# One burst of small-tile products per batch, at the boundary of its output tiles

## The chip, the cores and the metric

The kernel runs on one NeuronCore of a Trainium2 chip. The metric is the device time in microseconds. A NeuronCore has a matrix engine (TensorE, PE in the profile, with its weight loads listed as PEld), a vector engine (VectorE, DVE), a scalar engine (ScalarE, ACT), a general engine (GpSimd, POOL) and a queue engine for transfers (SyncE, SP). Products of TensorE land in PSUM, which has eight banks of 128 x 512 fp32 here; DVE and ACT copy them out.

## The reference

Two parts follow each other. A two-way cross attention between 512 tokens and 32 state rows, for 8 batches and 8 heads of width 64:

```python
scores  = x @ state.T / sqrt(D);  a  = softmax(scores);   xread = a  @ state   # 512 rows a batch
scores2 = state @ x.T / sqrt(D);  a2 = softmax(scores2);  sread = a2 @ x       # 32 rows a batch
attn = concat([xread, sread], axis=2)          # (B, H, 544, 64)
```

Then a feed-forward layer on all 8 x 544 rows of width 512 (the heads side by side): `gelu(rows @ w_in) @ w_out`, with an inner width of 2048.

## The kernel before

The kernel never forms `xread`. It multiplies the state with `w_in` first, `P = state @ w_in` for each head, and then takes `a @ P` for the hidden values. So a batch consists of:

- P: per batch four chunks of 512 hidden columns. The state of one head is 64 x 32, so a product uses a 64 x 32 part of the array (a "small tile"), and eight of them, four heads on each of two row halves, run side by side. A chunk fills two PSUM banks (t = 0, 1).
- `mm1`: the hidden tiles `hp`, full-array products, followed by a Gelu on ACT (16 per batch).
- `mm2`: the output tiles `op`, full-array products. A batch has four output tiles (j) of four quarters each (q), 16 steps; after q = 3, DVE copies the tile out (`evac`).
- `sread`: the read-out for the state rows, also on small tiles (128 x 32), and `srt`, its transpose.

PSUM is two pools of four banks:

```python
ps_f = ctx.enter_context(tc.tile_pool(name="ps_f", bufs=4, space=PSUM))
ps_o = ctx.enter_context(tc.tile_pool(name="ps_o", bufs=4, space=PSUM))
ctx.enter_context(tc.manual_schedule())
```

Each pool gives its banks out in turn, and each engine executes its instructions in the order of the program text. Here are the helpers that the change and the prediction touch:

```python
    def sread(b):
        A = atts[b]
        pool, tag = (ps_f, "f") if b < 2 else (ps_o, "op")
        A.sr = pool.tile([128, 2, 65], FP32, name="sr", tag=tag)
        for t in range(2):
            for j in range(SJ):
                for c in range(HC):
                    nc.tensor.matmul(
                        A.sr[32 * c:32 * c + 32, t, :],
                        lhsT=A.e[:, 2 * j + t, 32 * c:32 * c + 32],
                        rhs=A.xo[:, j, c, 1 + 65 * t:66 + 65 * t],
                        start=(j == 0),
                        stop=(j == SJ - 1),
                    )

    def sread_out(b):
        A = atts[b]
        A.srm = att.tile([128, 2, D], BF16, name="srm", tag="srm")
        flat = A.sr.rearrange("q t d -> q (t d)")
        inv = att.tile([128, 2], FP32, name="inv", tag="inv")
        nc.vector.reciprocal(out=inv, in_=flat[:, 0:130:129])
        nc.vector.tensor_tensor(
            out=A.srm,
            in0=flat[:, 1:129].rearrange("q (t d) -> q t d", t=2),
            in1=inv[:, :].to_broadcast((128, 2, D)),
            op=ALU.mult,
        )

    def pmat(b, fs, act=()):
        if b not in Ps:
            Ps[b] = att.tile([128, 2, d_ff], BF16, name="P", tag="P")
        pss = []
        for f in fs:
            pool, tag = (ps_o, "op") if b == 0 and f == 0 else (ps_f, "f")
            ps = [pool.tile([128, 512], FP32, name="p_ps", tag=tag) for t in range(2)]
            for c in range(HC):
                for t in range(2):
                    nc.tensor.matmul(
                        ps[t][32 * c:32 * c + 32, :],
                        lhsT=sbd[64 * t:64 * t + 64, b, c, 32 * t:32 * t + 32],
                        rhs=w_in_bf[64 * t:64 * t + 64, c, f * 512:(f + 1) * 512],
                        start=True,
                        stop=True,
                    )
            pss.append(ps)
        for f, ps in zip(fs, pss):
            for t in range(2):
                dst = Ps[b][:, t, f * 512:(f + 1) * 512]
                if t in act:
                    nc.scalar.copy(out=dst, in_=ps[t])
                else:
                    nc.vector.tensor_copy(out=dst, in_=ps[t])

    def mm1(b, m):
        if m == 0:
            gs[b] = gpool.tile([128, MC, S], BF16, name="g", tag="g")
        hp = ps_f.tile([128, S], FP32, name="hp", tag="f")
        for t in range(2):
            nc.tensor.matmul(
                hp,
                lhsT=Ps[b][:, t, m * 128:(m + 1) * 128],
                rhs=atts[b].AT[:, :, t, :],
                start=(t == 0),
                stop=(t == 1),
            )
        nc.scalar.activation(out=gs[b][:, m, :], in_=hp, func=AF.Gelu)

    ops = {}

    def evac(ps, rows):
        osb = opool.tile([128, d_model], FP32, name="osb", tag="osb")
        nc.vector.tensor_copy(out=osb, in_=ps)
        for r, src in rows:
            nc.sync.dma_start(out=r, in_=osb[src, :])

    # mm2(b, q, j), without its first lines
        if q == 0:
            ops[b, j] = ps_o.tile([128, d_model], FP32, name="op", tag="op")
        ps = ops[b, j]
        for m in range(4 * q, 4 * q + 4):
            nc.tensor.matmul(
                ps,
                lhsT=gs[b][:, m, j * 128:(j + 1) * 128],
                rhs=w_out_bf[:, m, :],
                start=(m == 0),
                stop=(m == MC - 1),
            )
        if q == 3:
            evac(ps, [(out_rows(b, j), slice(0, 128))])

    def M(*ms):
        for m in ms:
            mm1(m // MC, m % MC)

    def U(*us):
        for u in us:
            mm2(u // 16, u % 16 // 4, u % 4)
```

`scores(nb, half)` makes the scores of the next batch in `ps_f` and takes their exponential on ACT; `norm(nb, half)` is a sum, a reciprocal and a multiplication on DVE. The end of the prologue and the main loop:

```python
    # ... prologue cut
    M(16)
    pmat(1, (1,), act=(1,))
    U(13)
    M(17)
    U(14)
    pmat(1, (2,), act=(1,))
    M(18)
    U(15)
    M(19)


    u = 16
    for b in range(1, B):
        nb = b + 1
        for p in range(2 if b == 1 else 0, 8):
            k = 16 * b + 2 * p
            if p == (4 if b == 1 else 1) and nb < B:
                scores(nb, 0)
                scores(nb, 1)
                if b == 1:
                    norm(nb, 0)
                    norm(nb, 1)
            if b > 1 and p in (2, 3) and nb < B:
                norm(nb, p - 2)
            if p == (7 if b == 1 else 4) and nb < B:
                atr_dma(nb)
            if p == 5 and nb + 1 < B:
                begin(nb + 1)
                rearr(nb + 1)
                xtr_dma(nb + 1)
                rearr_ones(nb + 1)
            M(k, k + 1)
            if nb == B and p >= 4:
                for m in range(4 * p - 16, 4 * p - 12):
                    mm1_sr(m)
            while u < k - 4 - (b == 1 and p == 3):
                U(u)
                u += 1
            if b == 1 and p == 3:
                pmat(b, (3,), act=(1,))
                U(u)
                u += 1
            if b > 1 and p == 2:

                sread(b)
                pmat(b, (2, 3), act=(1,))
                sread_out(b)
            if p == 6 and nb < B:
                pmat(nb, (0, 1), act=(1,))
                if b + 3 < B:


                    nc.gpsimd.tensor_copy(out=hold, in_=Ps[nb][:, 0, 0:1])
                    load_x(b + 3)
            if p == 2 and b > 1 or p == 6 and nb < B:
                U(u, u + 1)
                u += 2
            if p == 3 and b > 1:
                srt(b)
```

The step U(u) runs four hidden tiles behind M, so the last output tile of batch b - 1 (u = 16 b - 1) ends in step p = 2 of batch b.

Of the kernel before, what the change touches and what calls it, by code (L numbers as in the profile page):

```python
# [9 lines left out]
FP32 = mybir.dt.float32  # L10
# [7 lines left out]
def kernel(  # L18
# [8 lines left out]
    nc = tc.nc  # L27

    B, H, S, D = x.shape
# [4 lines left out]
    HC = H // 2  # L34
# [10 lines left out]
    ps_f = ctx.enter_context(tc.tile_pool(name="ps_f", bufs=4, space=PSUM))  # L45
    ps_o = ctx.enter_context(tc.tile_pool(name="ps_o", bufs=4, space=PSUM))
# [5 lines left out]
    w_in_bf = persist.tile([128, HC, d_ff], BF16, name="w_in_bf")  # L52
    w_out_bf = persist.tile([128, MC, d_model], BF16, name="w_out_bf")
    ident = persist.tile([128, 128], BF16, name="ident")
    sbd = persist.tile([128, B, HC, 2 * NS], BF16, name="sbd")
# [6 lines left out]
    hold = persist.tile([128, 1], BF16, name="hold")  # L62
# [9 lines left out]
    for c in range(3):  # L72
# [5 lines left out]
        out=xbs[0].rearrange("p (t c) f -> p t c f", t=2)[:, :, 3, :], in_=x0_rows[:, :, 3, :]  # L78
# [22 lines left out]
    def load_x(b):  # L101
        xb = xin.tile([128, H, SJ * D], BF16, name="xb", tag="xb")
        nc.gpsimd.dma_start(out=xb, in_=xr[b])
        xbs[b] = xb
# [55 lines left out]
    def begin(b):  # L160
        A = Att()
        atts[b] = A
        A.x4 = x4s[b % 2]
        A.xo = xos[b % 2]
        A.xT = att.tile([128, SJ, HC, 128], BF16, name="xT", tag="xT")
        A.e = att.tile([128, SJ * 2, HC * NS], BF16, name="e", tag="e")
        A.a = att.tile([128, SJ * 2, HC * NS], BF16, name="a", tag="a")
# [117 lines left out]
    def norm(b, half):  # L285
        A = atts[b]
        G = SJ * 2
        hs = slice(64 * half, 64 * half + 64)
        e4 = A.e[:, :, hs].rearrange("p g (c n) -> p g c n", n=NS)
        cs = att.tile([128, G, 2], FP32, name="cs", tag="cs")  # L290
        nc.vector.reduce_sum(out=cs, in_=e4, axis=AX.X)  # L291
        ics = att.tile([128, G, 2], FP32, name="ics", tag="ics")
        nc.vector.reciprocal(out=ics, in_=cs)
        nc.vector.tensor_tensor(  # L294
            out=A.a[:, :, hs].rearrange("p g (c n) -> p g c n", n=NS),
            in0=e4,
            in1=ics[:, :, :].to_broadcast((128, G, 2, NS)),
            op=ALU.mult,
        )
# [20 lines left out]

    def sread(b):
        A = atts[b]
        pool, tag = (ps_f, "f") if b < 2 else (ps_o, "op")
        A.sr = pool.tile([128, 2, 65], FP32, name="sr", tag=tag)
        for t in range(2):
            for j in range(SJ):
                for c in range(HC):
# [20 lines that stand above are left out]
# [8 lines left out]

    Ps = {}

    def pmat(b, fs, act=()):
        if b not in Ps:  # L360
            Ps[b] = att.tile([128, 2, d_ff], BF16, name="P", tag="P")
        pss = []
        for f in fs:
            pool, tag = (ps_o, "op") if b == 0 and f == 0 else (ps_f, "f")
            ps = [pool.tile([128, 512], FP32, name="p_ps", tag=tag) for t in range(2)]
            for c in range(HC):
                for t in range(2):
                    nc.tensor.matmul(  # L368
                        ps[t][32 * c:32 * c + 32, :],
                        lhsT=sbd[64 * t:64 * t + 64, b, c, 32 * t:32 * t + 32],  # L370
                        rhs=w_in_bf[64 * t:64 * t + 64, c, f * 512:(f + 1) * 512],
                        start=True,
                        stop=True,
                    )
            pss.append(ps)
        for f, ps in zip(fs, pss):
            for t in range(2):
                dst = Ps[b][:, t, f * 512:(f + 1) * 512]
                if t in act:
                    nc.scalar.copy(out=dst, in_=ps[t])  # L380
                else:
                    nc.vector.tensor_copy(out=dst, in_=ps[t])  # L382


    def pmat00(t):
# [14 lines left out]
    gs = {}  # L400
# [14 lines that stand above are left out]
# [34 lines left out]
    def mm2(b, q, j):  # L449
        if b == B - 1 and j == SJ - 1:  # L450
            return
# [13 lines that stand above are left out]
# [30 lines left out]
# [7 lines that stand above are left out]
# [36 lines left out]

    M(0, 1, 2, 3)
    U(0, 1, 2)  # L540
    pmat(0, (1,), act=(1,))
    U(3)
    M(4, 5)
    state_prep(1, 2)
# [2 lines left out]
    xtr(1, (0, 1))  # L547
    xtr(1, (2, 3))
    sread(0)
    sread_out(0)  # L550
    M(7)
# [3 lines left out]
    U(4, 5)  # L555
    rearr_ones(1)
    U(6)
    pmat(0, (2,), act=(1,))
    norm(1, 0)
    norm(1, 1)  # L560
    U(7)
# [2 lines left out]
    sread_out(1)  # L564
    M(10, 11)
    U(8)
    pmat(0, (3,), act=(1,))
    U(9)
    atr(1)
    U(10)  # L570
# [1 line left out]
    srt(1)  # L572
    M(14, 15)
    U(11)
    pmat(1, (0,), act=(1,))
    begin(2)
    rearr(2)
    xtr_dma(2)
# [1 line left out]
    U(12)  # L580
    state_prep(2, B)
    M(16)
    pmat(1, (1,), act=(1,))
    U(13)
    M(17)
    U(14)
    pmat(1, (2,), act=(1,))
    M(18)
    U(15)
    M(19)  # L590


    u = 16
# [20 lines that stand above are left out]
            if nb == B and p >= 4:  # L614
                for m in range(4 * p - 16, 4 * p - 12):
                    mm1_sr(m)
            while u < k - 4 - (b == 1 and p == 3):
                U(u)
                u += 1
            if b == 1 and p == 3:  # L620
                pmat(b, (3,), act=(1,))
                U(u)
                u += 1
            if b > 1 and p == 2:

                sread(b)
                pmat(b, (2, 3), act=(1,))
                sread_out(b)
            if p == 6 and nb < B:
                pmat(nb, (0, 1), act=(1,))  # L630
                if b + 3 < B:


                    nc.gpsimd.tensor_copy(out=hold, in_=Ps[nb][:, 0, 0:1])  # L634
                    load_x(b + 3)
            if p == 2 and b > 1 or p == 6 and nb < B:
                U(u, u + 1)
                u += 2
            if p == 3 and b > 1:
                srt(b)  # L640
    while u < 16 * B - 4:
# [36 lines left out]
```

The softmax here doesn't subtract the row's maximum and nothing guards it: scores larger than these inputs give would overflow.

## Time and profile before

| | before |
|---|---|
| median of three runs | 217.58 us (217.23 to 217.58) |
| span of the profiled execution | 216.1 us |
| ACT busy | 122.3 us (57%) |
| DVE busy | 80.1 us (37%) |
| full products, output tiles (L456) | 496 products, 118.7 us |
| full products, hidden tiles (L407) | 256 products, 64.1 us |
| small products of P (L368) | 248 products, 10.8 us |
| small products of the read-out (L328) | 256 products, 3.4 us |

Busy time of TensorE counts overlapping products once; [...]the distance between starts, and not the length, is the cost of one more. A line of the timeline gives start, length, engine, source line, operation, what it writes and reads, the array part used, the shape and the count; in brackets stands the idle time before it, and what ended it. A stretch of main-loop batch takes 22.92 us in this profile (88.20 to 111.12, for one), and in it TensorE is busy throughout.

### The profile page before, as it was taken

Reading aid. Unit: us, or ns where it says so; the run is one execution under the profiler, and the core shown is the slowest. Engines: PE = TensorE matmul, PEld = TensorE weight load, DVE = VectorE, ACT = ScalarE, POOL = GpSimd, SP = SyncE. Lnnn points to the kernel's source line nnn. Section 1 sums busy time; section 2 is a strip of 40 time slices with the busy share of each in tenths; the row PEclk is TensorE's granted clock in tenths of the full one; section 3 lists DMA queues with packets and bytes.
Section 4 is the critical chain, followed back from the end, with each engine's and each line's share of the span. In section 5 each row is a group of like instructions: output and inputs, shape, how many; then the busy total and the mean of one; then the engine's idle time right before and its main releaser. Section 6 shows DMA issues by size and latency. Waiting matters only on the chain.

```text
span 216.1 us, 3993 instructions
## 1 busy us (share of the span) xinstructions
PE 210.0 (97%) x1663; PEld 101.2 (47%) x1663; DVE 80.1 (37%) x165; ACT 122.3 (57%) x217; POOL 43.5 (20%) x57
## 2 busy tenths in 40 slices
PE   8799999999999999999999999999999999999993
PEld 7535444444444444444544454444544444765442
DVE  4815664624248022912093107602580226000151
ACT  3754846677694447653965477547954444854000
POOL 7663303910133013301060014200000000000000
PEclk9999999999999999999999999999999999999999
DMA  7999999796543716570746672460222004000044
GB/s 182 183 188 205 205 191 147 188 203 49 61 117 119 146 8 89 197 131 15 102 167 55 121 96 98 133 113 2 91 106 49 3 39 158 3 0 0 14 127 153
DMA packets 38724, 22.98 MB, mean 106 GB/s; under 512 B 21937, under 2 KB 34481, under 8 KB 38705
## 3 DMA queue, kind: packets, MB, share of 16 engines
q0 software_dynamic: 13664, 8.23, 27.7%
q1 hardware_dynamic: 24352, 14.09, 25.9%
q10 hardware_dynamic: 688, 0.39, 0.6%
q8 instruction: 13, 0.21, 0.5%
q14 instruction: 7, 0.05, 0.1%
HBM read 17.30 MB, written 8.91 MB: 121 GB/s over the span
## 4 chain that ended last, share of the span: by engine, by line
PE 85%; DMA 11%; POOL 2%; issue 1%; ACT 0%; POOLq 0%
PE op L456 47%; PE hp L407 23%; DMA w_in_bf<-in_moe_w_in_dram 11%; PE p_ps L368 4%; PE hps L469 3%; PE ops L481 3%; PE opl L434 2%; PE pt L271 1%; PE sr L328 1%; POOL w_in_bf L89 1%; POOL xb L77 0%; POOL w_out_bf L99 0%; PE aT_ps L307 0%; PE srT L352 0%; PE st_ps L141 0%
## 5 line engine op out<-in xcount | busy, mean ns | idle before, releaser
L456 PE MATMUL op<-w_out_bf,g 128*128 128x512 bf16 x496 | 118.7, 379 | 0.2
L414 ACT ACTIVATE g<-hp 128x512 bf16<-128x512 f32 x128 | 67.3, 601 | 43.6 <-PE hp L407 43.5
L456 PEld LDWEIGHTS <-g 128*128 128x128 bf16 x496 | 46.8, 98 | 60.4 <-issue 6.2
L407 PE MATMUL hp<-AT,P 128*128 128x512 bf16 x256 | 64.1, 379 | 0.3 <-DVE AT L311 0.3
L382 DVE CAST P<-p_ps 128x512 bf16<-128x512 f32 x31 | 20.2, 684 | 53.6 <-PE p_ps L368 53.6
L407 PEld LDWEIGHTS <-P 128*128 128x128 bf16 x256 | 23.8, 98 | 27.9 <-issue 1.1
L420 DVE COPY osb<-op 128x512 f32<-128x512 f32 x31 | 20.9, 688 | 41.3 <-PE op L456 41.3
L380 ACT CAST P<-p_ps 128x512 bf16<-128x512 f32 x31 | 17.0, 588 | 24.3 <-PE p_ps L368 21.3
L175 POOL COPY x<-xb 128x1024 bf16<-128x1024 bf16 x12 | 12.1, 1040 | 32.3 <-DMA xb<-in_x_dram 27.3
L186 POOL COPY xo<-xb 128x1024 bf16<-128x1024 bf16 x12 | 12.2, 1045 | 9.1 <-PE sr L328 9.1
L368 PE MATMUL p_ps<-w_in_bf,sbd 64*32 64x512 bf16 x248 | 10.8, 382 | 0.1
L291 DVE TENSOR_REDUCE cs<-e 128x16 f32<-128x512 bf16 x14 | 9.5, 677 | 2.5 <-ACT e L278 2.5
L278 ACT ACT_TABLE_LOAD x7 | 9.0, 1283 | 1.9 <-issue 1.2
L294 DVE TENSOR_TENSOR a<-e,ics 128x512 bf16<-128x512 bf16 x14 | 9.7, 692 | 0.5
L420 DVE COPY osb<-ops 128x512 f32<-128x512 f32 x2 | 1.4, 692 | 22.5 <-PE ops L481 22.5
L634 POOL COPY hold<-P 128x1 bf16<-128x1 bf16 x4 | 0.8, 190 | 42.2 <-DVE P L382 42.2
L414 ACT ACT_TABLE_LOAD x7 | 9.0, 1283 | 0.1
L445 ACT COPY osb<-opl 128x128 f32<-128x128 f32 x1 | 0.3, 265 | 15.2 <-PE opl L434 15.2
L278 ACT ACTIVATE e<-pt 128x512 bf16<-128x512 f32 x14 | 7.6, 594 | 0.1
L469 PE MATMUL hps<-XSR,w_in_bf 128*128 128x256 bf16 x64 | 7.6, 273 | 0.0
L132 PE MATMUL warm_ps<-warm 128*128 128x128 bf16 x59 | 6.1, 270 | 1.0 <-DVE warm L75 1.0
L481 PE MATMUL ops<-w_out_bf,g_sr 128*128 128x512 bf16 x32 | 7.1, 379 | 0.0
(66 smaller groups left out, 106.1 us busy)
## 6 DMA issues: line engine op xcount, KB each, us to landing
out_dram<-osb SPq DMA_DIRECT2D x31, 256.0 KB, 2.4
xb<-in_x_dram POOLq DMA_DIRECT2D x7, 512.0 KB, 6.0
w_in_bf<-in_moe_w_in_dram POOLq DMA_DIRECT2D x8, 256.0 KB, 10.5
w_out_bf<-in_moe_w_out_dram POOLq DMA_DIRECT2D x4, 512.0 KB, 12.9
x0f<-in_x_dram SPq DMA_DIRECT2D x2, 256.0 KB, 3.5
out_dram<-osb SPq DMA_DIRECT2D x8, 64.0 KB, 1.7
x0f<-in_x_dram ACTq DMA_DIRECT2D x1, 256.0 KB, 4.3
st_bf<-in_state_dram POOLq DMA_DIRECT2D x1, 192.0 KB, 14.8
```

The source lines that it names most:

```text
L175: nc.gpsimd.tensor_copy(out=A.x4[:, :, :, 64 * t:64 * t + 64].rearrange("p j c d -> p c j d"), in_=src[:, t],)
L186: eng.tensor_copy(out=A.xo[:, :, c0:, 2 + 64 * t:66 + 64 * t].rearrange("p j c d -> p c j d"), in_=src[:, t, c0:],)
L278: nc.scalar.activation(out=A.e[:, :, 64 * half:64 * half + 64], in_=pt.rearrange("p j t c n -> p (j t) (c n)"), func=AF.Exp, scale=scale,)
L368: nc.tensor.matmul(ps[t][32 * c:32 * c + 32, :], lhsT=sbd[64 * t:64 * t + 64, b, c, 32 * t:32 * t + 32], rhs=w_in_bf[64 * t:64 * t + 64, c ...
L380: nc.scalar.copy(out=dst, in_=ps[t])
L382: nc.vector.tensor_copy(out=dst, in_=ps[t])
L407: nc.tensor.matmul(hp, lhsT=Ps[b][:, t, m * 128:(m + 1) * 128], rhs=atts[b].AT[:, :, t, :], start=(t == 0), stop=(t == 1),)
L414: nc.scalar.activation(out=gs[b][:, m, :], in_=hp, func=AF.Gelu)
L420: nc.vector.tensor_copy(out=osb, in_=ps)
L456: nc.tensor.matmul(ps, lhsT=gs[b][:, m, j * 128:(j + 1) * 128], rhs=w_out_bf[:, m, :], start=(m == 0), stop=(m == MC - 1),)
L469: nc.tensor.matmul(hp, lhsT=w_in_bf[:, c, m * 128:(m + 1) * 128], rhs=XSR[:, c, :], start=(c == 0), stop=(c == HC - 1),)
L481: nc.tensor.matmul(ps, lhsT=g_sr[:, m, s * 128:(s + 1) * 128], rhs=w_out_bf[:, m, :], start=(m == 0), stop=(m == MC - 1),)
```

## The change

P of a batch came in four chunks at two or more places: the first two chunks late in the batch before, the other two beside the read-out. The change collects four chunks in one run of small tiles, once per batch, at the step in which the output tiles of the last batch have ended and those of the next have not begun, so that the banks of `ps_o` can serve as well: two chunks in `ps_f`, two in `ps_o`, all eight banks. The read-out follows behind the chunks and takes a bank of `ps_f` in every batch. Batches 2 to 6 make their own last two chunks and the first two of the next batch in it; the first burst stands at the end of the prologue, and batch 7 has only two chunks left. It is meant to let the array change between whole and small tiles less often. With the burst, the output steps that were moved forward to stand behind each P run go back to their plain place, and the transfer of x for a later batch is held by a Gelu's result in place of a copy of P.

```diff
@@ -320,8 +320,7 @@
 
     def sread(b):
         A = atts[b]
-        pool, tag = (ps_f, "f") if b < 2 else (ps_o, "op")
-        A.sr = pool.tile([128, 2, 65], FP32, name="sr", tag=tag)
+        A.sr = ps_f.tile([128, 2, 65], FP32, name="sr", tag="f")
         for t in range(2):
             for j in range(SJ):
                 for c in range(HC):
@@ -356,30 +355,47 @@
 
     Ps = {}
 
-    def pmat(b, fs, act=()):
+    def p_mm(b, f, pool, tag):
         if b not in Ps:
             Ps[b] = att.tile([128, 2, d_ff], BF16, name="P", tag="P")
-        pss = []
-        for f in fs:
-            pool, tag = (ps_o, "op") if b == 0 and f == 0 else (ps_f, "f")
-            ps = [pool.tile([128, 512], FP32, name="p_ps", tag=tag) for t in range(2)]
-            for c in range(HC):
-                for t in range(2):
-                    nc.tensor.matmul(
-                        ps[t][32 * c:32 * c + 32, :],
-                        lhsT=sbd[64 * t:64 * t + 64, b, c, 32 * t:32 * t + 32],
-                        rhs=w_in_bf[64 * t:64 * t + 64, c, f * 512:(f + 1) * 512],
-                        start=True,
-                        stop=True,
-                    )
-            pss.append(ps)
-        for f, ps in zip(fs, pss):
+        ps = [pool.tile([128, 512], FP32, name="p_ps", tag=tag) for t in range(2)]
+        for c in range(HC):
             for t in range(2):
-                dst = Ps[b][:, t, f * 512:(f + 1) * 512]
-                if t in act:
-                    nc.scalar.copy(out=dst, in_=ps[t])
-                else:
-                    nc.vector.tensor_copy(out=dst, in_=ps[t])
+                nc.tensor.matmul(
+                    ps[t][32 * c:32 * c + 32, :],
+                    lhsT=sbd[64 * t:64 * t + 64, b, c, 32 * t:32 * t + 32],
+                    rhs=w_in_bf[64 * t:64 * t + 64, c, f * 512:(f + 1) * 512],
+                    start=True,
+                    stop=True,
+                )
+        return ps
+
+    def p_copy(b, f, ps):
+        dst = Ps[b][:, :, f * 512:(f + 1) * 512]
+        nc.scalar.copy(out=dst[:, 0, :], in_=ps[0])
+        nc.vector.tensor_copy(out=dst[:, 1, :], in_=ps[1])
+
+    def pmat(b, f):
+        p_copy(b, f, p_mm(b, f, ps_f, "f"))
+
+
+
+
+    def burst(chunks, b_read=None):
+        done = []
+        for i, (b, f) in enumerate(chunks):
+            pool, tag = (ps_f, "f") if i < 2 else (ps_o, "op")
+            done.append((b, f, p_mm(b, f, pool, tag)))
+        for x in done[:2]:
+            p_copy(*x)
+        if b_read is not None:
+            sread(b_read)
+        for x in done[2:3]:
+            p_copy(*x)
+        if b_read is not None:
+            sread_out(b_read)
+        for x in done[3:]:
+            p_copy(*x)
 
 
     def pmat00(t):
@@ -538,7 +554,7 @@
 
     M(0, 1, 2, 3)
     U(0, 1, 2)
-    pmat(0, (1,), act=(1,))
+    pmat(0, 1)
     U(3)
     M(4, 5)
     state_prep(1, 2)
@@ -555,7 +571,7 @@
     U(4, 5)
     rearr_ones(1)
     U(6)
-    pmat(0, (2,), act=(1,))
+    pmat(0, 2)
     norm(1, 0)
     norm(1, 1)
     U(7)
@@ -564,7 +580,7 @@
     sread_out(1)
     M(10, 11)
     U(8)
-    pmat(0, (3,), act=(1,))
+    pmat(0, 3)
     U(9)
     atr(1)
     U(10)
@@ -572,7 +588,7 @@
     srt(1)
     M(14, 15)
     U(11)
-    pmat(1, (0,), act=(1,))
+    pmat(1, 0)
     begin(2)
     rearr(2)
     xtr_dma(2)
@@ -580,14 +596,13 @@
     U(12)
     state_prep(2, B)
     M(16)
-    pmat(1, (1,), act=(1,))
+    pmat(1, 1)
     U(13)
     M(17)
     U(14)
-    pmat(1, (2,), act=(1,))
-    M(18)
+    M(18, 19)
     U(15)
-    M(19)
+    burst([(1, 2), (1, 3), (2, 0), (2, 1)])
 
 
     u = 16
@@ -614,28 +629,16 @@
             if nb == B and p >= 4:
                 for m in range(4 * p - 16, 4 * p - 12):
                     mm1_sr(m)
-            while u < k - 4 - (b == 1 and p == 3):
+            while u < k - 4:
                 U(u)
                 u += 1
-            if b == 1 and p == 3:
-                pmat(b, (3,), act=(1,))
-                U(u)
-                u += 1
-            if b > 1 and p == 2:
-
-                sread(b)
-                pmat(b, (2, 3), act=(1,))
-                sread_out(b)
-            if p == 6 and nb < B:
-                pmat(nb, (0, 1), act=(1,))
-                if b + 3 < B:
-
-
-                    nc.gpsimd.tensor_copy(out=hold, in_=Ps[nb][:, 0, 0:1])
-                    load_x(b + 3)
-            if p == 2 and b > 1 or p == 6 and nb < B:
-                U(u, u + 1)
-                u += 2
+            if p == 2 and b > 1:
+                burst([(b, 2), (b, 3)] + ([(nb, 0), (nb, 1)] if nb < B else []), b)
+            if p == 6 and b + 3 < B:
+
+
+                nc.gpsimd.tensor_copy(out=hold, in_=gs[b][:, 12, 0:1])
+                load_x(b + 3)
             if p == 3 and b > 1:
                 srt(b)
     while u < 16 * B - 4:
```

## The prediction

> **What bounds the kernel now.** I read the page's busy times first, then what TensorE waits for, then its instructions in order of time, and last the two engines that empty PSUM, around one batch boundary.
>
> ```profile
> span 216.1 us, 3993 instructions
> PE 210.0 (97%) x1663; PEld 101.2 (47%) x1663; DVE 80.1 (37%) x165; ACT 122.3 (57%) x217; POOL 43.5 (20%) x57
> ```
>
> TensorE (PE) is busy 97% of the span, at a granted clock of 9 tenths or more in all 40 slices; its list of waits for other engines, on matmuls, holds 2.3 us, all of it in the first 12 us. So the order of TensorE's own stream is the time. What that stream pays beyond the columns it streams is seen in the timeline of TensorE (start us, length us, engine, line, operation, count) around the boundary of batches 2 and 3 of the output:
>
> ```profile
> 85.58 1.03 PE L407 MATMUL hp<-AT,P 128*128 128x512 bf16 x4
> 86.44 1.89 PE L456 MATMUL op<-w_out_bf,g 128*128 128x512 bf16 x8
> 88.27 0.43 PE L328 MATMUL sr<-xo,e 128*32 128x65 bf16 x32
> 88.62 0.63 PE L368 MATMUL p_ps<-w_in_bf,sbd 64*32 64x512 bf16 x16
> 89.18 1.90 PE L456 MATMUL op<-w_out_bf,g 128*128 128x512 bf16 x8
> ...
> 97.88 1.89 PE L456 MATMUL op<-w_out_bf,g 128*128 128x512 bf16 x8
> 99.70 0.63 PE L368 MATMUL p_ps<-w_in_bf,sbd 64*32 64x512 bf16 x16
> 100.26 1.90 PE L456 MATMUL op<-w_out_bf,g 128*128 128x512 bf16 x8
> ```
>
> Lengths overlap; starts are what to subtract. Four full products take 86.44 - 85.58 = 0.86 us, 0.2157 each, so the eight from 97.88 end their issue at 99.61. The small tiles start at 99.70: entering costs 0.09 to 0.10 us. The 16 small products (eight run side by side, so two chunks need 2 x 0.2157 = 0.43 us) take 100.26 - 99.70 = 0.56: leaving costs 0.13. A run of a single chunk, in batch 1, pays the same twice:
>
> ```profile
> 38.59 1.03 PE L456 MATMUL op<-w_out_bf,g 128*128 128x512 bf16 x4
> 39.55 0.41 PE L368 MATMUL p_ps<-w_in_bf,sbd 64*32 64x512 bf16 x8
> 39.89 0.60 PE L407 MATMUL hp<-AT,P 128*128 128x512 bf16 x2
> ```
>
> 38.59 + 0.863 = 39.45, entry 0.10; 39.89 - 39.55 = 0.34 against 0.216 streamed, exit 0.125. One run of small tiles therefore costs about 0.22 us however many chunks are in it.
>
> A check that nothing else is in a batch: from 88.27 the next state read-out starts at 111.19, 22.92 later. 96 full products make 20.71, scores 0.46, the two P runs 1.12, read-out 0.355, its transpose 0.06, two entries 0.20: 22.90. TensorE has no stall in a batch today.
>
> **What the Trainium skill says.** "TensorEngine Tiling (Array Packing)", Tiling Modes, Key Properties: changing the tiling mode, and not just the tile, drains TensorE. It gives no figure; the trace agrees, with 0.10 in and 0.13 out. The same page, Performance Considerations, PSUM Bottleneck: tiling speeds TensorE up but not the emptying of PSUM, which can then limit. Here a chunk streams in 0.216 us and is emptied by two copies that take 0.588 (ACT) and 0.684 us (DVE), so the page's warning fits as soon as chunks follow one another. "TensorE: Matmul & The Clock Gate", Part 1, puts warm products of 512 columns at 215.7 ns start to start; the trace has 0.2157 us. Its Part 3, The mechanism, says that matmuls start and end in program order: a product that waits for its bank holds up all behind it. No stall in steady state here shows that.
>
> **The change, part by part.** The work is the same: 248 P products in this helper, 31 ACT and 31 DVE copies of P. What moves is their place.
>
> (a) Removed switches. In batches 2 to 6 the P run late in the batch (the one at 99.70) disappears into the one at the boundary. Before: 0.10 + 0.355 + 0.56, and 0.10 + 0.56 = 1.675 us. After: entry 0.10, four chunks 0.863 and a switch 0.13, read-out 0.355 = 1.45. Gain 0.23 each, 5 x 0.23 = 1.15. In batch 1 the two single runs (1,2) and (1,3) and the pair for batch 2 become one burst: 0.44 + 0.44 + 0.66 = 1.54 against 0.10 + 0.863 + 0.13 = 1.09, gain 0.45. Sum -1.60 us. Batch 7 keeps its one run.
>
> (b) New waits on PSUM. The burst takes all eight banks in 0.86 us: chunks 0 and 1 the four of the first pool, chunks 2 and 3 the four that the output tiles have just ended in. Chunk 3 lands in the banks of output tiles 2 and 3 of the batch before, and tile 3 is what the eight products ahead of the burst end with. DVE and ACT over the same stretch:
>
> ```profile
> 86.39 0.68 DVE L291 TENSOR_REDUCE cs<-e 128x16 f32<-128x512 bf16 x1
> 87.10 0.25 DVE L293 RECIPROCAL ics<-cs 128x16 f32<-128x16 f32 x1
> 87.39 0.69 DVE L294 TENSOR_TENSOR a<-e,ics 128x512 bf16<-128x512 bf16 x1
> 88.00 1.28 DVE L420 COPY osb<-op 128x512 f32<-128x512 f32 x2
> 89.20 1.27 DVE L382 CAST P<-p_ps 128x512 bf16<-128x512 f32 x2
> ```
>
> ```profile
> 82.99 1.28 ACT L278 ACT_TABLE_LOAD   x1 [1.22 <-issue]
> 84.29 1.09 ACT L278 ACTIVATE e<-pt 128x512 bf16<-128x512 f32 x2
> 85.39 1.28 ACT L414 ACT_TABLE_LOAD   x1
> 86.68 2.06 ACT L414 ACTIVATE g<-hp 128x512 bf16<-128x512 f32 x4
> 89.13 1.07 ACT L380 CAST P<-p_ps 128x512 bf16<-128x512 f32 x2 [0.38 <-PE p_ps L368]
> ```
>
> The softmax steps for the next batch sit ahead of the two output copies on DVE, so the second copy ends at 88.00 + 1.28 = 89.28. A release reaches TensorE about 0.06 us after the releaser ends:
>
> ```profile
> 10.97 0.42 DVE L311 COPY AT<-aT_ps 128x512 bf16<-128x512 bf16 x1
> 11.45 2.05 PE L407 MATMUL hp<-AT,P 128*128 128x512 bf16 x8 [0.29 <-DVE AT L311]
> ```
>
> (11.39 to 11.45.) Put the burst where the read-out starts today, 88.27. Chunk 0 at 88.27. Chunk 1 at 88.49, but its second bank is that of the last Gelu, which ends at 86.68 + 2.06 = 88.74: it starts at 88.80. Chunk 2 at 89.02. Chunk 3 would start at 89.23 now, and waits for 89.28 + 0.06 = 89.34. Without waits it is 88.27 + 0.65 = 88.92. Stall 0.42 us in each of batches 2 to 6: 5 x 0.42 = +2.10. The Gelu's wait is inside it.
>
> Behind it nothing more is late. The read-out would start at 89.34 + 0.22 + 0.13 = 89.69, and its bank (chunk 0, ACT copy from about 88.8, ends 89.4) is free. The next hidden product, at about 90.04, needs the DVE copy of chunk 0 (89.20 to 89.84): free. The output tiles after it take chunk 2's banks at 90.9 and 91.8, copied by ACT by 90.4 and by DVE by 91.1: free. The read-out's transpose, at 92.6, needs its normalized rows by 91.5.
>
> In batch 1 no softmax is ahead on DVE: the last tile's copy starts 0.10 after the burst (0.20 after the last product's issue ends, as at 179.39 and 179.60 in batch 7) and ends 0.69 later; chunk 3, due at 0.65, starts at 0.85. Stall +0.20.
>
> In batch 7 there are only two chunks, and the read-out, which had a bank of the output pool, must now wait until ACT has copied chunk 0. A single run's ACT copy starts 0.51 after the run (39.55, copy at 40.05), so it ends at 0.51 + 0.59, and the read-out starts at 1.16 in place of 0.56. Stall +0.60; before there was none.
>
> (c) The transfer of x for three batches on is now released by a Gelu and not by a copy of P, some 3 us earlier. The GpSimd copy behind it ended at 86.4 for an x whose transposing transfer starts at 93.88, so 7 us were in hand already: 0.
>
> Sum: -1.60 + 2.10 + 0.20 + 0.60 = +1.30 us; 217.58 + 1.30 = 218.9.
>
> **The rivals.** *The switches alone count.* If output copies were done before chunk 3 asks, -1.6 us remains: 216.0. For it: the switch costs are seen plainly. Against: the copy of tile 3 ends 0.36 us later than an unhindered chunk 3 would start, and the program order keeps it so. *The waits spread.* If each stall delays the copies behind it and the read-out or the next hidden products wait too, 0.3 us more in each of six batches gives 220.7. For it: ACT has four P copies in a row behind the Gelus, 2.2 us; against: each bank's next user, followed above, comes 0.2 us or more after its copy. *The small tiles already hide the stall*, since TensorE's queue loads weights ahead: the drain on entry would still be paid, and only some 0.1 us per batch would be saved of the stall: 218.4.
>
> **Range and chances.** The two large terms have opposite signs and depend on starts read to about 0.05 us; six batches times 0.1 us is 0.6, and the first batches and batch 7 add about as much. I take 217.4 to 219.9. Two per cent is 4.35 us, more than any rival gives: faster 0.02, same 0.95, slower 0.03.
>
> **What would show it.** In the changed profile: the batch period, 22.92 now, at about 23.1; one run of 32 small products that takes about 1.4 us from its first start to the read-out (1.0 if there is no wait), with a gap before the last eight and DVE's output copy named as the releaser; the period without a burst unchanged. In batch 7, the read-out some 1.15 us after the first small product, released by ACT. If the burst takes 1.0 us, (b) is wrong and the time falls to about 216; if the period grows beyond 23.3, I missed a wait behind the burst.

## The result

The changed kernel takes 218.74 us (median of four runs, 218.45 to 219.59), the kernel before 217.46 us in the runs beside it: a ratio of 1.0066, 95% interval 1.0037 to 1.0096, well inside the two per cent that the prediction calls "same". That is 1.28 us by the medians; the prediction was +1.30 us on the median it was given, 218.9. The interval stands for 0.8 to 2.1 us, so that the two figures agree to 0.02 us is luck; the stretches of the two traces below are the finer test.

The page of the changed kernel, busy times:

```profile
span 217.8 us, 3990 instructions
PE 210.7 (97%) x1663; PEld 103.2 (47%) x1663; DVE 78.9 (36%) x165; ACT 122.5 (56%) x217; POOL 43.3 (20%) x57
```

TensorE is still the bound; its busy time can't show the answer, since the wait sits inside the small tiles' own length (1.47 us of PE "busy" in the first line below). The timeline of TensorE around the boundary of batches 2 and 3, columns as before:

```profile
88.69 1.47 PE L364 MATMUL p_ps<-w_in_bf,sbd 64*32 64x512 bf16 x32
90.09 0.43 PE L327 MATMUL sr<-xo,e 128*32 128x65 bf16 x32
90.45 1.04 PE L423 MATMUL hp<-AT,P 128*128 128x512 bf16 x4
...
111.80 1.47 PE L364 MATMUL p_ps<-w_in_bf,sbd 64*32 64x512 bf16 x32
```

One run of small tiles per batch instead of two, and the read-out 1.40 us behind its first product; four chunks and a switch would take 1.0. The batch is 111.80 - 88.69 = 23.11 us, against 22.92. Where the 0.4 us is lost shows in the weight loads of the same stretch (PEld):

```profile
88.69 0.14 PEld L364 LDWEIGHTS <-sbd 64*32 64x32 bf16 x10 [0.42 <-issue]
89.23 0.31 PEld L364 LDWEIGHTS <-sbd 64*32 64x32 bf16 x16 [0.40 <-issue]
89.76 0.10 PEld L364 LDWEIGHTS <-sbd 64*32 64x32 bf16 x6 [0.22 <-issue]
```

A chunk has eight loads. In each group that ends at a gap in this trace there are two more than whole chunks (10 here, 26 in the next batch), so I read a gap as a wait of the chunk that has had two loads. Ten loads are then chunk 0 and two of chunk 1; at 89.23 chunk 1 runs on, at 89.76 chunk 3 does. The last Gelu and DVE's two output copies tell what these times are:

```profile
87.11 2.06 ACT L430 ACTIVATE g<-hp 128x512 bf16<-128x512 f32 x4
88.42 1.28 DVE L436 COPY osb<-op 128x512 f32<-128x512 f32 x2
```

The last Gelu ends at 89.17, and chunk 1 follows 0.06 later. The second copy ends at 89.70; chunk 3 follows 0.06 later. One batch on, there is one gap only, and it ends with the copy again (111.53 + 1.28 = 112.81, and 0.06):

```profile
111.80 0.56 PEld L364 LDWEIGHTS <-sbd 64*32 64x32 bf16 x26 [0.42 <-issue]
112.87 0.10 PEld L364 LDWEIGHTS <-sbd 64*32 64x32 bf16 x6 [0.51 <-issue]
111.53 1.28 DVE L436 COPY osb<-op 128x512 f32<-128x512 f32 x2
```

So the wait that took the place of the switch looks to be DVE's copy of output tile 3. The profile's own list names only "issue" for these gaps, so this rests on the times, and on the experiments below.

The first burst, in batch 1, and the short one of batch 7:

```profile
41.77 1.26 PE L364 MATMUL p_ps<-w_in_bf,sbd 64*32 64x512 bf16 x32
42.96 1.90 PE L423 MATMUL hp<-AT,P 128*128 128x512 bf16 x8
...
180.66 0.62 PE L364 MATMUL p_ps<-w_in_bf,sbd 64*32 64x512 bf16 x16
181.77 0.43 PE L327 MATMUL sr<-xo,e 128*32 128x65 bf16 x32 [0.49 <-ACT P L375]
```

The first takes 1.19 us, and in batch 7 the read-out starts 1.11 after the first small product and is released by ACT's copy of P.

Cutting the two traces at the same instructions gives the account:

| stretch | before | after | difference |
|---|---|---|---|
| run of chunk (1,1) to scores of batch 3 (first burst) | 22.66 | 22.40 | -0.26 |
| scores of batch 3 to scores of batch 7 (four bursts) | 91.69 | 92.44 | +0.75 |
| scores of batch 7 to the small tiles of batch 7 (one burst) | 28.20 | 28.38 | +0.18 |
| from there to the first hidden tile of the state rows | 4.44 | 4.99 | +0.55 |
| sum | | | +1.22 |

The two profiled spans differ by 1.7 us because the first 37 us, which the change leaves nearly alone, were 0.50 us longer in this execution: TensorE waited 1.0 us for x at 7 to 8 us, where the kernel before did not, and 0.2 us for `w_in` where it had waited 0.7. In the profiles of the other changed kernels the same point lies between 36.3 and 37.3 us (37.44 here), so this belongs to the execution.

### The profile page after: what moved, and what is told of

Same layout as the page of the kernel before. It is cut to its first block, busy times and chain, and to the rows that moved or that the text cites. A ratio compares the mean times of both kernels' runs of the same rounds, so it can differ in the third digit from the quotient of the medians.

```text
span 217.8 us, 3990 instructions
## 1 busy us (share of the span) xinstructions
PE 210.7 (97%) x1663; PEld 103.2 (47%) x1663; DVE 78.9 (36%) x165; ACT 122.5 (56%) x217; POOL 43.3 (20%) x57
## 4 chain that ended last, share of the span: by engine, by line
PE 90%; ACT 3%; DMA 3%; DVE 1%; issue 1%; POOLq 0%
PE op L472 49%; PE hp L423 25%; PE p_ps L364 5%; PE hps L485 3%; PE ops L497 3%; DMA xb<-in_x_dram 3%; ACT g L430 2%; PE opl L450 2%; PE pt L271 1%; PE sr L327 1%; PE xT_ps L211 1%; ACT L430 1%; ACT P L375 1%; PE aT_ps L307 0%; DVE a L258 0%
## 5 line engine op out<-in xcount | busy, mean ns | idle before, releaser
L430 ACT ACTIVATE g<-hp 128x512 bf16<-128x512 f32 x128 | 68.7, 601 | 56.6 <-PE hp L423 56.5
L472 PEld LDWEIGHTS <-g 128*128 128x128 bf16 x496 | 48.0, 98 | 58.2 <-ACT g L430 1.9
L423 PE MATMUL hp<-AT,P 128*128 128x512 bf16 x256 | 65.8, 379 | 0.3 <-DVE AT L311 0.3
L375 ACT CAST P<-p_ps 128x512 bf16<-128x512 f32 x31 | 16.3, 596 | 11.7 <-PE p_ps L364 11.7
L364 PEld LDWEIGHTS <-sbd 64*32 64x32 bf16 x248 | 3.5, 89 | 8.9 <-issue 7.9
```

What stands on the lines that cost most here:

```text
L364: nc.tensor.matmul(ps[t][32 * c:32 * c + 32, :], lhsT=sbd[64 * t:64 * t + 64, b, c, 32 * t:32 * t + 32], rhs=w_in_bf[64 * t:64 * t + 64, c ...
L375: nc.scalar.copy(out=dst[:, 0, :], in_=ps[0])
L423: nc.tensor.matmul(hp, lhsT=Ps[b][:, t, m * 128:(m + 1) * 128], rhs=atts[b].AT[:, :, t, :], start=(t == 0), stop=(t == 1),)
L472: nc.tensor.matmul(ps, lhsT=gs[b][:, m, j * 128:(j + 1) * 128], rhs=w_out_bf[:, m, :], start=(m == 0), stop=(m == MC - 1),)
```

## Experiments

Four theories were to be told apart. The prediction's: in a burst, chunk 3 waits for DVE's copy of the last output tile, with a wait of chunk 1 for the last Gelu hidden inside it. Rival A: only one of the two is real. Rival B: there is no wait, small tiles in such a run are simply slow. And under all of them: is the switch worth 0.22 us at all?

"Burst" below is the time from the first small product to the first product of the read-out, in batches 2 to 6; "batch" is the distance from one such place to the next.

| run | burst, us | batch, us | time, us | ratio to before (95%) |
|---|---|---|---|---|
| before | two runs | 22.92 | 217.4 | 1 |
| changed | 1.40 to 1.41 | 23.11 | 218.74 | 1.0066 (1.0037 to 1.0096) |
| b: softmax steps behind the burst | 1.30 in batch 3, else 1.18 to 1.19 | 22.89 to 22.90, 23.01 behind batch 3's burst | 217.79 | 1.0014 (1.0008 to 1.0021) |
| c: scores earlier | 1.40 to 1.41 | 23.11 | 218.75 | 1.0060 (1.0045 to 1.0075) |
| d: both | 1.19 | 22.90 | 217.54 | 1.0006 (1.0000 to 1.0013) |
| e: batch 7's old bank | 1.40 | 23.11 | 218.44 | 1.0051 (1.0036 to 1.0067) |
| f: d and e | 1.19 | 22.90 | 217.13 | 0.9991 (0.9985 to 0.9998) |
| g: before, one run more a batch | three runs | 23.15 | 218.76 | 1.0063 (1.0049 to 1.0077) |
| h: f, a hidden tile ahead of the burst | 1.23 | 22.94 | 217.50 | 1.0001 (0.9993 to 1.0010) |
| i: only the first burst | two runs | 22.92 | 217.09 | 0.9987 (0.9980 to 0.9994) |
| j: read-out behind chunk 0 | - | 22.82 | 216.93 | 0.9972 (0.9964 to 0.9980) |
| k: j, a hidden tile ahead | - | 22.92 | 217.29 | 0.9995 (0.9988 to 1.0002) |
| l: j, batch 7's outputs first | - | 22.82 | 216.54 | 0.9967 (0.9954 to 0.9980) |

**What a run of small tiles costs (g).** In the kernel before, a run of two chunks becomes two runs of one, with the same products; one of the two output steps that followed now stands between them (the lines that take it from there are left out):

```diff
             if p == 6 and nb < B:
-                pmat(nb, (0, 1), act=(1,))
+                pmat(nb, (0,), act=(1,))
+                U(u)
+                pmat(nb, (1,), act=(1,))
```

> The kernel before, with the pair of chunks late in batches 1 to 6 split into two runs of one chunk, with an output step between them: six more runs of small tiles, the same products. Theory (a run costs its two switches, whatever is in it): 0.22 each, +1.3 us over the kernel before, about 218.8. Rival (the switch is hidden by weight loads ahead, and the gain of the change was never there): below +0.3, 217.7.

Measured: 218.76 us, ratio 1.0063, some 1.4 us for six more runs; the batch grows from 22.92 to 23.15 us, 0.23 for a run:

```profile
88.58 0.43 PE L328 MATMUL sr<-xo,e 128*32 128x65 bf16 x32
...
100.01 0.41 PE L368 MATMUL p_ps<-w_in_bf,sbd 64*32 64x512 bf16 x8
100.35 1.04 PE L456 MATMUL op<-w_out_bf,g 128*128 128x512 bf16 x4
101.32 0.41 PE L368 MATMUL p_ps<-w_in_bf,sbd 64*32 64x512 bf16 x8
101.66 1.04 PE L456 MATMUL op<-w_out_bf,g 128*128 128x512 bf16 x4
...
111.73 0.43 PE L328 MATMUL sr<-xo,e 128*32 128x65 bf16 x32
```

The switch is a real cost, a run of one chunk pays it as a run of two does, and the gain the change was made for exists.

**Which wait holds the burst (b, c, d).** Two moves, each alone and together. b moves softmax steps on DVE behind the burst:

```diff
-            if b > 1 and p in (2, 3) and nb < B:
-                norm(nb, p - 2)
+            if b > 1 and p == 3 and nb < B:
+                norm(nb, 0)
+                norm(nb, 1)
```

> The changed kernel with the first softmax half of the next batch moved behind the burst on DVE (both halves then stand one step later). Burst means: first small product to first product of the read-out, 1.40 us in batches 2 to 6 of the changed kernel. Theory (two waits, one inside the other): the output copy of tile 3 now ends 0.79 after the burst starts, but the last Gelu still holds chunk 1 until 0.53, so chunk 3 runs at 0.96 and the burst takes 1.29; five batches save 0.55, about 218.2 us. Rival A (only the DVE copy holds the burst): 1.20, as in batch 1, about 217.7. Rival B (no wait, the small tiles themselves take this long): 1.40, 218.7.

c makes the next batch's scores one step earlier, so that ACT has done its table loads and Gelus before the burst:

```diff
-            if p == (4 if b == 1 else 1) and nb < B:
+            if p == (4 if b == 1 else 0) and nb < B:
                 scores(nb, 0)
                 scores(nb, 1)
```

> The changed kernel with the scores of the next batch (and their exponentials and two table loads on ACT) one step earlier; DVE's order unchanged. Theory (two waits, one inside the other): the Gelu wait is gone, but the output copy behind the softmax steps still ends 1.01 after the burst starts, so nothing is seen: burst 1.40, about 218.7 us. Rival A (the Gelu is what holds the burst): 1.20, about 217.7. Rival B (no wait): 1.40 here, and 1.40 also when both are moved.

d has both:

> Both moves at once: scores one step earlier, softmax steps on DVE behind the burst. Theory: the output copy of tile 3 alone is left, ending 0.79 after the burst starts: chunk 3 at 0.85, burst 1.20, five batches save 1.0 us against the changed kernel, about 217.7. Rival B (no wait): 1.40, 218.7. If neither wait is left in any form: 1.0, about 216.7.

c changes nothing: burst 1.40 to 1.41 in all five batches, 218.75 us. So the Gelu isn't what holds the burst. With b the burst falls to 1.18 or 1.19 in four of five batches, and with d in all five: DVE's copy behind the softmax steps was the wait, and rival B is out. The hidden wait, though, exists in batch 3 only; in the other four batches rival A is right, with DVE's copy as the one wait. The weight loads of b, batch 3 and then batch 4:

```profile
87.37 0.14 PEld L364 LDWEIGHTS <-sbd 64*32 64x32 bf16 x10 [0.42 <-issue]
87.91 0.42 PEld L364 LDWEIGHTS <-sbd 64*32 64x32 bf16 x22 [0.40 <-issue]
...
110.38 0.54 PEld L364 LDWEIGHTS <-sbd 64*32 64x32 bf16 x26 [0.42 <-issue]
111.23 0.11 PEld L364 LDWEIGHTS <-sbd 64*32 64x32 bf16 x6 [0.31 <-issue]
```

In batch 3 chunk 1 stops until 87.91, 0.06 after the last Gelu (87.85, four Gelus of 2.06 us from 85.79 on), then all runs through. In batch 4 the first 24 products run through, and only chunk 3 stops, until 0.85 after the start. The difference is where ACT's table load starts: 0.47 us after the scores in batch 3 of the changed kernel (83.42 and 82.95), 0.79 us ahead of them in batch 4 (105.27 and 106.06). Why it starts late in batch 3 alone, no run shows. So b came out at 217.79, where the two nested waits said 218.2 and the copy alone 217.7.

What is left in d is the copy in its earliest place, as in batch 1:

```profile
87.50 1.26 PE L364 MATMUL p_ps<-w_in_bf,sbd 64*32 64x512 bf16 x32
88.69 0.43 PE L327 MATMUL sr<-xo,e 128*32 128x65 bf16 x32
```

```profile
87.61 0.69 DVE L436 COPY osb<-op 128x512 f32<-128x512 f32 x1 [0.17 <-PE op L472]
```

The copy ends at 88.30; chunk 3's loads go on at 88.36, 0.86 after the start of the burst (expected 0.85).

**Batch 7 (e).** The read-out of the last batch goes back into a bank of the output pool:

```diff
-        A.sr = ps_f.tile([128, 2, 65], FP32, name="sr", tag="f")
+        pool, tag = (ps_f, "f") if b < B - 1 else (ps_o, "op")
+        A.sr = pool.tile([128, 2, 65], FP32, name="sr", tag=tag)
```

> The changed kernel, but the read-out of the last batch takes a bank of the output pool, as in the kernel before. Theory: the gap of 0.49 us ahead of this read-out, put down to ACT's copy of P, is the bank and nothing else; in batch 7 the read-out starts 0.56 after the first small product in place of 1.11, and the time falls by 0.55 to about 218.2 us. Rival (the read-out must wait for something else there, as its own exponentials or x): it stays at 1.11, 218.7.

Measured: 218.44 us, 0.30 less by the medians, not 0.55. With four runs each the two intervals overlap, so the traces must say what was gained. The read-out gains what was said, but something behind it takes part back:

```profile
180.49 0.62 PE L365 MATMUL p_ps<-w_in_bf,sbd 64*32 64x512 bf16 x16
181.04 0.43 PE L328 MATMUL sr<-xo,e 128*32 128x65 bf16 x32
181.60 1.02 PE L424 MATMUL hp<-AT,P 128*128 128x512 bf16 x4
```

```profile
180.96 1.07 ACT L376 CAST P<-p_ps 128x512 bf16<-128x512 f32 x2 [1.44 <-PE p_ps L365]
```

The read-out starts 0.55 after the first small product, in place of 1.11; so the gap in the changed kernel was the bank. But the hidden product starts 0.56 behind the read-out, where 0.36 is usual, at 181.60, 0.05 after ACT's first copy is done (180.96 and 0.59). The wait for a bank of the first pool moved from the read-out to the hidden product, and the stretch gains 0.38 (185.65 - 180.66 = 4.99 against 185.10 - 180.49 = 4.61). In the kernel before, two output steps, which need no bank of that pool, stood there.

**Both together (f), and the first burst alone (i).**

> Both moves, and the read-out of batch 7 in a bank of the output pool. Theory: the switches saved in batches 2 to 6 (0.23 each) are paid back by 0.20 of wait each, batch 1 keeps its 0.25, batch 7 is as before: 0.3 to 0.4 us below the kernel before, about 217.1. Rival (the moves cost elsewhere what they save): no better than 217.5.

i keeps the first burst and lets the later batches be as before: read-out in the output pool, two runs of two chunks in batches 2 to 6, each followed by two output steps. Two small things stay as in the changed kernel: the transfer of x is released by a Gelu, and ACT empties the first bank of a chunk and DVE the second, which was the other way round before.

> The burst at the end of the prologue alone, with everything else as in the kernel before: the read-out in the output pool, two runs of two chunks in batches 2 to 6. Theory: batch 1 saves two runs (0.45) and waits 0.20 on its last output copy: 0.25 below the kernel before, about 217.2 us. Rival (the first burst pays as little as the later ones): 217.5.

Measured 217.13 and 217.09 us: both 0.1% faster than the kernel before, each interval below 1. The stretch of the first burst keeps its gain (22.40 us in i, as in the changed kernel). In f the five later bursts, with the Gelu's wait gone and DVE's copy as early as in batch 1, win 0.02 us a batch (22.90 against 22.92), and batch 7 still pays 0.17 (4.61 against 4.44). So the gain of f is that of the first burst.

**The same burst without the wait for the output copy (h).** Here one hidden tile is put between the last output tile and the burst, and the banks are taken in another order, so that DVE's copy is done (88.14) before its bank is asked for (88.21):

```diff
-            M(k, k + 1)
+            turn = b > 1 and p == 2 and nb < B
+            M(*((k,) if turn else (k, k + 1)))
             # ... the output steps
+            if turn:
+                M(k + 1)
-            pool, tag = (ps_f, "f") if i < 2 else (ps_o, "op")
+            first = i in (0, 3) if turn else i < 2
+            pool, tag = (ps_f, "f") if first else (ps_o, "op")
```

The copies of chunk 3 come second in order.

> As the run with both moves and the bank for batch 7, and in batches 2 to 6 one hidden tile is put between the last output tile and the burst, so that DVE's output copy is done before its banks are asked for; banks are taken in the order first pool, output pool, output pool, first pool. Theory (with all eight banks in use the read-out must wait until chunk 0 is copied out): the burst still takes 1.2 to 1.3 us, now released by ACT's copy of P, no better than the run with both moves. Rival (only the output copy was in the way): 1.0 to 1.08, and some 0.7 us less than the run with both moves.

Measured: burst 1.23, 217.50 us. The weight loads, and below them ACT:

```profile
87.78 0.54 PEld L365 LDWEIGHTS <-sbd 64*32 64x32 bf16 x26 [0.42 <-issue]
88.53 0.10 PEld L365 LDWEIGHTS <-sbd 64*32 64x32 bf16 x6 [0.22 <-issue]
89.01 0.30 PEld L328 LDWEIGHTS <-e 128*32 128x32 bf16 x32 [0.37 <-ACT P L376]
```

```profile
87.89 0.60 ACT L434 ACTIVATE g<-hp 128x512 bf16<-128x512 f32 x1 [1.56 <-PE hp L427]
88.38 2.22 ACT L376 CAST P<-p_ps 128x512 bf16<-128x512 f32 x4
```

The burst began at 87.78. Chunk 3, now in the first pool, stops until 88.53, 0.04 after the Gelu of the extra tile ends (88.49); that is 0.10 later than its own sequence. ACT's first copy starts 0.60 after the burst, behind that Gelu, and takes some 0.59: the read-out, which has no free bank of eight, starts at 89.01, 0.04 after it ends, where chunk 3 and the switch (0.34) would have let it start at 88.87. The profile names this copy as the releaser; it names it in d too, but there the loads stood idle 0.23 us ahead of the read-out, here 0.37. With the tile wait gone, the emptying of chunk 0 is the wait that ends last, as the theory said.

**A burst that doesn't ask too early (j, k).** The read-out goes second, into a bank of the output pool that is free, and the second half of chunk 3 goes into the bank of chunk 0, which is empty by then. Moves b and c and the old bank for batch 7 are in it.

```diff
+    def burst_mid(b, a=0):
+        c0 = p_mm(b, 2, ps_f, "f")
+        sread(b)
+        c1 = p_mm(b, 3, ps_f, "f")
+        c2 = p_mm(b + 1, 0, ps_o, "op")
+        p_copy(b, 2, c0, a)
+        sread_out(b)
+        c3 = p_mm(b + 1, 1, ps_o, "op", split=True)   # t = 1 in ps_f
+        # ... copies of c1, c2, c3
```

> As the run with both moves and the bank for batch 7, but in batches 2 to 6 the read-out stands behind chunk 0, in a bank of the output pool, and the second half of chunk 3 takes chunk 0's first bank, which ACT has emptied 1.16 after the burst starts. Theory (a burst must not ask for a bank before 1.16 that chunk 0 still holds): chunk 0 0.22 and a switch 0.13, read-out 0.355, chunks 1 and 2 0.43 bring chunk 3 to 1.14, which then waits 0.03 in place of 0.20; one switch more (0.13) is paid; the next hidden product may wait 0.1 for DVE's copy of chunk 0. From first small product to next hidden product 1.4 to 1.5 where the run with both moves has 1.55; five batches: 216.6 to 217.0 us. Rival (the extra switch between the two kinds of small tiles costs what the wait did): 217.1, as the run with both moves.

```profile
87.44 0.41 PE L366 MATMUL p_ps<-w_in_bf,sbd 64*32 64x512 bf16 x8
87.78 0.43 PE L328 MATMUL sr<-xo,e 128*32 128x65 bf16 x32
88.14 0.84 PE L366 MATMUL p_ps<-w_in_bf,sbd 64*32 64x512 bf16 x24
88.91 1.04 PE L437 MATMUL hp<-AT,P 128*128 128x512 bf16 x4
```

0.34, 0.36 and 0.77 us: the first and the last are their streamed columns (0.22 and 0.65) and one switch, the read-out takes what it takes in the kernel before, and the 24 weight loads of chunks 1 to 3 run without a gap. The sum is 1.47 (expected 1.4 to 1.5), the batch 22.82, and the time 216.93 us, ratio 0.9972 (0.9964 to 0.9980): faster than both kernels, and than f, whose interval lies above this one.

k adds h's extra hidden tile and has DVE empty chunk 0's first bank (`a=1`).

> The same, with one hidden tile between the last output tile and the burst, and chunk 0's first bank emptied by DVE in place of ACT. Theory: DVE is past the output copy by then, so the next hidden product doesn't wait any more, and ACT's Gelu of the extra tile costs chunk 1 at most 0.03: 1.4 from first small product to next hidden product, 216.3 to 216.6 us. Rival (ACT, with a Gelu and four copies, becomes the wait): no better than the run without the extra tile.

This one missed: 217.29 us, 1.57 from first small product to next hidden product, the batch 22.92. Its weight loads and DVE:

```profile
88.62 0.10 PEld L366 LDWEIGHTS <-sbd 64*32 64x32 bf16 x6 [0.17 <-issue]
```

```profile
87.86 0.69 DVE L378 CAST P<-p_ps 128x512 bf16<-128x512 f32 x1
```

DVE's copy ends at 88.55, and chunk 3 goes on at 88.62, 1.23 after the start at 87.39, where TensorE's own sequence would have been there at about 1.13. ACT, with a shorter copy, released that bank in time in j. k changes two things at once; this gap belongs to the second, the copy given to DVE, and the wait for ACT that the rival named is not what is seen. The wait that k was to take away had cost nothing: in j the next hidden product starts at 88.91, when chunk 3 and the switch are over, and DVE's copy (88.16 + 0.68 = 88.84, and 0.06) is done at that same moment.

**The outputs of batch 7 first (l).** j, and after batch 7's small tiles the two output steps again:

```diff
                 else:
                     burst([(b, 2), (b, 3)], b)
+                    U(u, u + 1)
+                    u += 2
```

> As the run with the read-out behind chunk 0, and in batch 7 the two output steps follow the burst at once, as in the kernel before. In the run with batch 7's old bank, the read-out had gained 0.56 us, but the next hidden product then started 0.20 later than the read-out's end and switch allow, just when ACT's copy of chunk 0 was done. Theory (a bank of the first pool): the output steps need no bank of that pool, so the 0.20 goes: from batch 7's first small product to the first hidden tile of the state rows 4.4 in place of 4.6, 216.7 us. Rival (the hidden product waits for something that is late anyway): 4.6, 216.9.

Measured: 4.44 us from the first small product of batch 7 (178.10) to the first hidden tile of the state rows (182.54), as in the kernel before, where j has 4.61 (178.25 to 182.86); 216.54 us, ratio 0.9967 (0.9954 to 0.9980). The output step follows the read-out 0.36 later:

```profile
178.66 0.43 PE L328 MATMUL sr<-xo,e 128*32 128x65 bf16 x32
179.02 1.90 PE L486 MATMUL op<-w_out_bf,g 128*128 128x512 bf16 x8
```

The 0.17 is gone, as the bank theory says. The run alone can't exclude another cause, since it starts the hidden product 1.5 us later and would hide anything else that was a little late; but the program text leaves only the bank: the columns of P that this product reads were made a batch earlier, and it takes the bank that ACT's copy of chunk 0 frees. The intervals of j and l overlap, so that l beats j rests on the trace; that it beats both kernels is measured.

## Why the prediction was right, and where it wasn't

**The view.** That TensorE's stream is the time, with no stall in a batch, held: the four stretches of the table account for +1.22 of the 1.28 us.

**(a) Removed switches.** Predicted 0.22 to 0.23 us a run; g measured 0.23. In batch 1 the gain of 0.45 less the wait of 0.20 should give -0.25; measured -0.26.

**(b) Chunk 3 and DVE's copy.** Predicted: chunk 3 at 1.07, read-out at 1.42, net +0.19 a batch. The trace has 1.07, 1.40 and +0.19, and b, c and d show by moving it that it is this copy, made late by the softmax steps ahead of it. The sign named for it, DVE as the releaser in the profile, did not appear. "Behind it nothing more is late" held: from the read-out to the next hidden product it is 0.36 us, where the read-out took 0.35 to the small tiles behind it before.

**"The Gelu's wait is inside it"** failed as a general statement: read from batch 3, where chunk 1 did wait until 0.54, it isn't so in the others. In the sum it cost nothing, since the longer wait hides it; it made the expectation for b 0.4 us too long. One batch had been taken for all, and its ACT timeline was the odd one. The profile of the kernel before shows this already: in the next batch ACT's table load starts at 104.71, ahead of the scores at 105.45, and the last Gelu is over 0.73 us before the read-out at 111.19.

```profile
104.71 1.28 ACT L278 ACT_TABLE_LOAD   x1
108.40 2.06 ACT L414 ACTIVATE g<-hp 128x512 bf16<-128x512 f32 x4
```

**Batch 7.** Predicted +0.60, by a copy starting 0.51 after the run; measured +0.55 and the copy starts 0.47 after it (181.13 and 180.66). e shows that it is the bank, and that a second wait lies behind it, which the prediction did not look for in batch 7: free the read-out, and the next hidden product asks for the same copy. In the changed kernel that second wait is hidden by the first.

**(c) The transfer of x.** No stall of TensorE answers to it. It was not tried alone, but i contains it, and came out 0.27 us below the kernel before where the first burst alone was to give 0.25.

**The rivals.** "The switches alone count" would have been 216.0, 1.6 us below the kernel before; the changed kernel is far from it. l, the best version, which has no wait in the later bursts, wins about half: it pays one more switch in each of five (0.12 to 0.13) and keeps the wait of the first (0.20). "The waits spread", 0.3 us more a batch, is out: behind the burst the next hidden product follows the read-out by 0.36 us, and the batch grew by 0.19. "The small tiles already hide the stall" would have left about 0.1 us less a batch, 218.4 us; the batch period decides against it, while the median, 218.74, would not have been clear of it.

## What to carry to other kernels

When switches of the array's tile form are worth saving, count how soon the run asks for each PSUM bank as well: merging the runs merges the demand, and here a stream of 0.22 us a chunk outran copies of 0.6 to 0.7 us once no bank was left over. Look in the timeline of the copying engine for what is ahead of the one copy that frees the bank, and order the run so that the late bank is asked for last and what needs few banks comes early; in this kernel that was worth one more switch. Read a stage from several iterations before saying that a wait is in each.

## What was not expected of the hardware

Going from one small-tile form to another (64 x 32 to 128 x 32 and back) costs about as much as going to the whole array: in j chunk 0 takes 0.34 us up to the read-out, of which 0.22 is streamed, and 0.34 to 0.35 before a whole-array product in the kernel before; the read-out takes 0.35 to 0.36 us before small tiles (88.27 to 88.62 in the kernel before) and 0.36 before a whole-array product (90.09 to 90.45 in the changed one). And ACT's table load, which looked tied to the scores in batch 3, starts 0.8 us ahead of them in the next batch; what decides this stays open.
